# Planning a fifth slot early, casting the first slot's weights later, and reading the last routing first

## The chip, the cores and the metric

One core of a Trainium2 chip runs the whole program in one launch. The time is device microseconds of one execution, and the median of several is given. The engines are TensorE (PE, its weight loads apart as PEld), VectorE (DVE), ScalarE (ACT), GpSimd (POOL) and SyncE (SP), whose queue issues nearly all loads.

## The reference

Three stages follow one another.

1. Linear attention with a forget gate: 4 x 8 heads, 768 steps, head size 48. `state = f * state + k v^T`, `y = q state`.
2. A dense feed-forward over the 3072 tokens of 384 numbers: `h = x @ w_in` (384 x 2048), `g = softplus(h)`, `x2 = g @ w_out` (2048 x 384).
3. A mixture of eight experts. `logits = x2 @ w_gate + bias[modality]`; the largest names one expert of each token. A token's result is `p * (relu(x2 @ w1[e]) @ w2[e])`, with w1[e] 384 x 1024, w2[e] 1024 x 384 and p its softmax weight.

Counted with the reference on its inputs, the tokens by expert are 17, 281, 476, 430, 193, 956, 154, 181 after the first 2688 and 20, 327, 542, 487, 219, 1097, 167, 213 after all 3072.

## The kernel before, in words

**Tiling.** The tokens run in eight groups of 384 (NG = 8). Attention and dense layer are interleaved: a dense step `s` is one of 16 slices of 128 hidden units of one group, so there are 128 steps, numbered 0 to 127; step 112 is the first of the last group. Where exactness counts, a matrix of 32-bit numbers is split into a rounded part and a remainder (h and l, hi and lo): ScalarE casts, VectorE subtracts, and TensorE makes three matmuls of what would be one.

**A dense step** (the last group, steps 112 to 127). `up` (L573) makes 9 matmuls into PSUM, 384 columns each. `softplus` follows: abs (ACT L578), exp (ACT L579), two operations on DVE (L584, L585), the logarithm (ACT L586), two more on DVE (L587, L588); then `act2`: hi (ACT L612) and lo (DVE L613). `down` (L653) adds 9 matmuls into three banks `x2ps`, for the step two before.

**Routing.** When a group's last `down` is done, `route1` (L671 to L679) reads each bank j of `x2ps`: the logits `lg` on DVE (L674) and the row itself, `rows`, on ACT for j = 0 and 2 (L679) and on DVE for j = 1 (L677). `route2` then finds the expert and the row number and scatters the rows on POOL into a buffer `xs` in HBM that has a region for each expert (L724).

**Slots.** Afterwards the rows are worked off in slots: up to 256 rows of one expert with its whole weights. One slot is 8 blocks of `m_up` (block f: 9 matmuls L1115 into one of four PSUM buffers, relu `hh` on ACT L1117, remainder `hl` on DVE L1118), two halves of `m_down` (24 matmuls each, L1138) into a bank of `x2ps`, and `m_out`, which scales the result (ACT L1147) and scatters it on POOL (L1148). `m_T` transposes a slot's rows on TensorE (L1097) and splits them (ACT L1099, DVE L1100).

**Two plans.** The first NPRE slots are planned in step 116 (`plan_first`) from the seven groups that are complete by then; only whole blocks of 256 rows are taken. The rest is planned in slot 2 (`plan_rest`), after the last group's rows and the pad rows (`pad_rows`, L1209, eight transfers on POOL): NA slots of 256 rows and NSTAT in all, beside one "pair" slot. A branch at the end runs if more slots than that are needed. The numbers reach the loads by register reads on SP: the expert of a slot (L994), its first row (L982), the pair's experts (L1026). The rows of slot s are loaded by L984 into one of three buffers.

**Weights of a slot.** Eight transfers of 384 KB on SP (`raw`, L1008), in turn a quarter of w1 and a quarter of w2, each followed by a cast (ACT L1009) and a subtraction (DVE L1010). The first slot has two `raw` buffers, the others six. The first slot's transfers and casts are named in steps 117 to 124, one in each step; those of a later slot while the slot before it runs, beside its blocks. The weights of two slots fit at a time.

**Order.** Instructions are named in program order, which is their priority. A planner simulates the engines with its own costs and fixes each engine's order: the first ready by priority goes next. `follow(a, b)` puts a behind b in that order, without a wait on the chip. `at(s, f)` names f's work in step s. Each engine then runs its list strictly in order. After the dense steps the blocks 0 to 2 of slot 0 are named among the last parts of the dense layer, as `TAIL = "uaduue"` says (u: a block of slot 0, a: `act2` of the last step, d and e: the last two `down`). The buffers `lg` and `rows` of the last routing come from a pool (`gq`) that opens when the pool of the dense layer (`gp`), which also holds slot 0's operands, is closed.

```
    m_slots(seq, {(0, 3): final, (1, 2): lambda: route2(NG - 1), (1, 4): ready, (2, 2): then, (6, 3): limits})
```

This says that the last `route1` (`final`) is named behind block 3 of slot 0, and `plan_rest` (`then`) behind block 2 of slot 2.

Of the kernel before, what the change touches and what calls it, by code (L numbers as in the profile page):

```python
# [7 lines left out]
F32 = mybir.dt.float32  # L8
# [3 lines left out]
AF = mybir.ActivationFunctionType  # L12
ALU = mybir.AluOpType
# [5 lines left out]
NT, DM, DFF = 3072, 384, 2048  # L19
E, FE = 8, 1024  # L20
TG = 384
NG = NT // TG
# [2 lines left out]
NB = 16  # L25
SLOT = 256
CAP = NT + SLOT
NPRE = 4
NA = 8
NREST = 17  # L30
NSTAT = 10
HALF = 64
PAIRAT = 12
LEAN = 16
# [1 line left out]
PRE = 4  # L36
# [3 lines left out]
TAIL = "uaduue"  # L40
WPOS = 1
PADROW = E * CAP
PAIR0, PAIR1 = NF, NF * (NG - 1)
RW = 388
BIG = 65536.0
WS = 256.0
# [5 lines left out]
def moe_chain(ctx, tc, qT, kT, fT, vp, w_in, w_out, mod, w_gate, mbias, w1, w2, out):  # L52
    nc = tc.nc
# [23 lines left out]
    x2ps = [ps_x.tile([128, 512], F32, name=f"x2ps{j}") for j in range(3)]  # L77


    def follow(ins, other):  # L80

        tc.add_manual_dep(ins.ins, other.name,
                          mybir.DependencyInfo(mybir.DependencyClass.NoSync, mybir.DependencyReason.DATA),
                          reason="first steps first")
# [4 lines left out]
    marks = {}  # L89
# [315 lines left out]
    biasT = cp.tile([128, 24, 8], F32, name="biasT")  # L405
# [170 lines left out]
    def softplus(g, h, e, w, lean=False):  # L576

        ins = nc.scalar.activation(e, h, AF.Abs).ins  # L578
        nc.scalar.activation(e, e, AF.Exp, scale=-1.0)  # L579
        if lean:  # L580
            nc.scalar.activation(w, e, AF.Copy, bias=1.0)
            nc.vector.scalar_tensor_tensor(w, w, 1.0, e, op0=ALU.subtract, op1=ALU.subtract)
        else:
            nc.vector.tensor_scalar(w, e, 1.0, -1.0, op0=ALU.add, op1=ALU.add)  # L584
            nc.vector.tensor_tensor(w, w, e, op=ALU.subtract)  # L585
        nc.scalar.activation(e, e, AF.Ln, bias=1.0)  # L586
        nc.vector.scalar_tensor_tensor(e, h, 0.0, e, op0=ALU.max, op1=ALU.add)  # L587
        nc.vector.tensor_tensor(g, e, w, op=ALU.subtract)  # L588
        return ins
# [77 lines left out]
    def sm(nm, shape, dt=F32):  # L667
        return gp.tile(shape, dt, tag=nm, name=nm)

    def route1(G, j):  # L670
        if j == 0:  # L671
            rt[G] = {"lg": sm("lg", [128, 3, 8]), "rows": gp.tile([128, 3, RW], F32, tag="rows", name="rows", bufs=1)}
        lg, rows = rt[G]["lg"], rt[G]["rows"]
        nc.vector.scalar_tensor_tensor(lg[:, j, :], x2ps[j][:, DM:DM + 8], 1.0 / WS, biasT[:, 3 * G + j, :],  # L674
                                       op0=ALU.mult, op1=ALU.add)
        if j == 1:
            nc.vector.tensor_scalar(rows[:, j, 0:DM], x2ps[j][:, 0:DM], 1.0 / WS, None, op0=ALU.mult)  # L677
        else:
            nc.scalar.activation(rows[:, j, 0:DM], x2ps[j][:, 0:DM], AF.Copy, scale=1.0 / WS)  # L679

    def route2(G):
        d = rt[G]
# [52 lines left out]

    used = cp.tile([NREST, 8], F32, name="used")

    def pick(nm, num, w, offs):


        end, beg, oh, tmp, off = (cp.tile([NREST, w], F32, name=f"{x}{nm}") for x in ("end", "beg", "soh", "stmp", "off"))
        sel, row = (cp.tile([NREST, 1], F32, name=f"{x}{nm}") for x in ("sel", "row"))
        woff, roff = (cp.tile([NREST, 1], I32, name=f"{x}{nm}") for x in ("woff", "roff"))
        nc.vector.tensor_tensor_scan(end, num, zer[:, 0:w], 0.0, op0=ALU.add, op1=ALU.add)
# [10 lines left out]
        nc.vector.tensor_reduce(row, tmp, axis=AX.X, op=ALU.add)  # L755
        nc.vector.tensor_scalar(roff, row, float(PADROW), None, op0=ALU.add)
        return woff, roff, beg, end

    def counts(sh, add):
        p = ps_r.tile([128, 512], F32, tag="r", name="r")  # L760
        nc.tensor.matmul(p[:, 0:8], onesb, runb, start=True, stop=True)
        cf, ci = cp.tile([NREST, 8], F32, name=f"cf{sh}"), cp.tile([NREST, 8], I32, name=f"ci{sh}")
        nc.vector.tensor_copy(cf, p[0:NREST, 0:8])
        nc.vector.tensor_scalar(ci, cf, float(add), None, op0=ALU.add)
# [9 lines left out]
    def plan_first():  # L774
# [4 lines left out]
        woff, roff, beg, _ = pick("0", num, 8, rows0[:, 0:8])  # L779
        taken(used, beg, num, NPRE)  # L780
        return woff, roff
# [10 lines left out]
    def halves(num, offs):  # L792
# [15 lines left out]
        nc.vector.tensor_copy(pw, ph[:, :, 0])  # L808
        nc.vector.tensor_scalar(pr, ph[:, :, 1], float(PADROW), None, op0=ALU.add)
        return pw, pr  # L810

    def plan_rest():
# [12 lines left out]
        nc.vector.tensor_tensor(beg, end, num, op=ALU.subtract)  # L825
        taken(n16[:, 0:8], beg, num, NA)
        nc.vector.tensor_tensor(num, used, n16[:, 0:8], op=ALU.add)
# [11 lines left out]
    def limits():  # L839
# [4 lines left out]
        nc.vector.tensor_copy(nsl[:, 0:1], end)  # L844
        nc.vector.tensor_scalar(far, end, float(-NSTAT), 0.0, op0=ALU.add, op1=ALU.max)
        nc.vector.tensor_reduce(flm, fl, axis=AX.X, op=ALU.max)
# [34 lines left out]
    def at(s, f):  # L881
        extra.setdefault(s, []).append(f)
# [32 lines left out]
    for u in range(4, 33):  # L915
        G, j = divmod(u, 4)
        t = 3 * u - 10 if u < 8 else 4 * u - 19
# [74 lines left out]
    def m_weights(s, woff, i, whole):  # L992

        wo = nc.sync.value_load(woff[i:i + 1, 0:1], min_val=0, max_val=E - 1)  # L994
        pl = m1p[s % 2]
        names = ("w1h", "w1l", "w2h", "w2l")
        w1h, w1l, w2h, w2l = wts[s] = [pl.tile([128, 3 * FE], F32R, tag=n, name=n) for n in names]
        ops = []
        for n in range(4):
            for src, hi, lo in ((w1, w1h, w1l), (w2, w2h, w2l)):  # L1000
                def op(n=n, src=src, hi=hi, lo=lo):
                    c = slice(768 * n, 768 * n + 768)
                    rows = src[bass.ds(wo, 1), :, c].rearrange("o p f -> p (o f)")
                    if whole and src is w1:
                        nc.sync.dma_start(hi[:, c].bitcast(F32), rows)
                        return
                    t = rawp.tile([128, 768], F32, tag="raw", name="raw")
                    nc.sync.dma_start(t, rows)  # L1008
                    nc.scalar.copy(hi[:, c], t)  # L1009
                    nc.vector.tensor_tensor(lo[:, c], t, hi[:, c].bitcast(F32), op=ALU.subtract)  # L1010
                ops.append(op)
        return ops

# [88 lines left out]
    def m_up(s, f):  # L1102
        d = sl[s]
        t = d["t"]
        w1h, w1l = (t.rearrange("p (k f) -> p k f", k=3) for t in wts[s][0:2])
        if f == 0:
            d["hh"] = mp.tile([128, NF2, SLOT], F32R, tag="hh", name="hh")
            d["hl"] = mp.tile([128, NF2, SLOT], F32R, tag="hl", name="hl")
        if d["n"] == 2:
            hp = ps_h.tile([128, TG], F32, tag="h", name="h")  # L1110
            fs = slice(128 * f, 128 * f + 128)
            n = 0
            for kd in range(3):
                for w, x in ((w1h, 0), (w1h, 1), (w1l, 0)):
                    nc.tensor.matmul(hp[:, 0:SLOT], w[:, kd, fs], t[x][:, kd, :], start=(n == 0), stop=(n == 8))  # L1115
                    n += 1
            nc.scalar.activation(d["hh"][:, f, :], hp[:, 0:SLOT], AF.Relu)  # L1117
            nc.vector.scalar_tensor_tensor(d["hl"][:, f, :], hp[:, 0:SLOT], 0.0, d["hh"][:, f, :].bitcast(F32),  # L1118
                                           op0=ALU.max, op1=ALU.subtract)
        elif f % 2 == 0:  # L1120
            w1f = wts[s][0].bitcast(F32).rearrange("p (k f) -> p k f", k=3)
            hp = ps_h.tile([128, 2, 128], F32, tag="h", name="h")
            for i in range(2):
                fs = slice(128 * (f + i), 128 * (f + i) + 128)
                for kd in range(3):
                    nc.tensor.matmul(hp[:, i, :], w1f[:, kd, fs], t[:, kd, :], start=(kd == 0), stop=(kd == 2))
            hh, hl = d["hh"][:, f:f + 2, 0:128], d["hl"][:, f:f + 2, 0:128]
            nc.scalar.activation(hh, hp, AF.Relu)
            nc.vector.scalar_tensor_tensor(hl, hp, 0.0, hh.bitcast(F32), op0=ALU.max, op1=ALU.subtract)
# [25 lines left out]

    seq = [("first", i, 2) for i in range(NPRE)] + [("rest", i, 2 if i < NA else 1) for i in range(NSTAT)]
    seq.insert(PAIRAT, ("pair", 0, 1))
    more = [("rest", i, 1) for i in range(NSTAT, NREST)]
    plans = {}
# [46 lines left out]
    def pad_rows(e):  # L1206
# [5 lines left out]
            tc.declare_no_dep(ins, other, reason="rows of different experts")  # L1212
        pads.append(ins)

    def pre():
        plans["first"] = plan_first()
        for i in range(NPRE - 1):
            m_load(i, "first", i, 2)
        for n, op in enumerate(m_fetch(0, seq[0])):
            at(16 * (NG - 1) + PRE + 1 + n, op)  # L1220

    ffn(0, 16 * (NG - 1) + 3)
    for p in (ap1, ap2, ps_r, ps_h):
# [166 lines left out]
    with tc.If(rare > 0):  # L1390
        nv = nc.values_load(nsl[0:1, 0:1], min_val=0, max_val=NREST)
        with tc.If(nv > NSTAT):
            more = [(len(seq) + x, it) for x, it in enumerate(more)]
# [53 lines left out]
```

## Time and profile before

| | us |
|---|---|
| median of 3 runs (lowest, highest) | 816.93 (815.72, 817.48) |
| the profiled execution | 814.61 |
| its span | 812.9 |
| PE busy | 786.5 (97%) |
| PE weight loads busy | 730.8 (90%) |
| DVE busy | 633.5 (78%) |
| ACT busy | 530.4 (65%) |
| POOL busy | 64.9 (8%) |

The granted clock of TensorE is at its full level (2.4 GHz) in all slices of the page. Times in the views are microseconds from the span's start. The last group's dense steps lie at about 500 to 566 us, slot 0 runs until about 581 us, and each later slot of 256 rows takes some 17.6 us. A matmul's end is modelled, and the next one starts before it; idle time of an engine that isn't the bound costs nothing.

### The profile page before, as it was taken

What the parts mean: (1) busy time and instruction counts of PE and PEld (TensorE: products, weight loads), DVE (VectorE), ACT (ScalarE), POOL (GpSimd) and SP (SyncE); (2) the same over time, 40 slices, a digit from 0 to 9 for tenths busy, and PEclk for the clock granted to TensorE, in tenths of its full rate; (3) what the DMA queues carried; (4) which work ended last, traced back from release to release, by engine and by line L of the source; (5) the groups of instructions that cost most, each with busy time, mean ns of one, the idle gap of its engine ahead of it and who ended that gap; (6) DMA issues with size and microseconds to landing.
All of it is one profiled execution on the core that took longest, in us unless ns stands there. A gap on an engine that the chain in (4) does not pass through costs nothing.

```text
span 812.9 us, 16010 instructions
## 1 busy us (share of the span) xinstructions
PE 786.5 (97%) x5878; PEld 730.8 (90%) x5878; DVE 633.5 (78%) x1265; ACT 530.4 (65%) x1057; POOL 64.9 (8%) x86
## 2 busy tenths in 40 slices
PE   4899999999999999999999999999999999999997
PEld 4656568999999999999999999989999999999987
DVE  6899999998888888888888866888886766666131
ACT  5787797767766676777676665566775656655242
POOL 2000000200010010010010010100042111000010
PEclk9999999999999999999999999999999999999999
DMA  8794221321132132122221010055598976673980
GB/s 292 255 328 140 59 67 44 91 73 54 45 95 58 45 98 58 51 85 61 62 75 38 23 38 8 30 161 171 200 352 298 309 226 216 213 225 119 366 311 16
DMA packets 53976, 110.84 MB, mean 136 GB/s; under 512 B 7655, under 2 KB 27930, under 8 KB 53888
## 3 DMA queue, kind: packets, MB, share of 16 engines
q1 hardware_dynamic: 48768, 96.61, 37.2%
q0 software_dynamic: 4160, 12.67, 4.2%
q8 instruction: 48, 0.79, 0.4%
q10 hardware_dynamic: 960, 0.44, 0.2%
q14 instruction: 40, 0.33, 0.1%
HBM read 91.92 MB, written 13.65 MB: 130 GB/s over the span
## 4 chain that ended last, share of the span: by engine, by line
PE 49%; DVE 23%; ACT 10%; issue 10%; DMA 7%; SPq 1%; POOL 1%; POOLq 0%; DVEq 0%; ACTq 0%
PE x2ps L653 11%; PE h L573 11%; PE x2ps L1138 10%; PE h L1115 10%; DVE l L637 3%; DVE w L636 2%; DMA raw<-in_w_dram 2%; ACT e L633 1%; DVE f L110 1%; PE r L206 1%; ACT e L622 1%; DVE lo L640 1%; DVE am L214 1%; DVE l L639 1%; ACT r L623 1%
## 5 line engine op out<-in xcount | busy, mean ns | idle before, releaser
L573 PE MATMUL h<-xh,wih 128*128 128x384 f32 x336 | 118.4, 352 | 1.2 <-DVE e L587 1.2
L653 PE MATMUL x2ps<-woh,hi 128*128 128x392 f32 x336 | 115.3, 343 | 1.8 <-ACT hi L612 1.5
L653 PE MATMUL x2ps<-wol,hi 128*128 128x392 f32 x336 | 114.5, 341 | 0.0
L573 PE MATMUL h<-xh,wil 128*128 128x384 f32 x336 | 113.5, 338 | 0.0
L653 PE MATMUL x2ps<-woh,lo 128*128 128x392 f32 x336 | 113.4, 341 | 0.0
L573 PE MATMUL h<-xl,wih 128*128 128x384 f32 x336 | 113.3, 337 | 0.0
L1115 PE MATMUL h<-thl,w1h 128*128 128x256 f32 x528 | 96.5, 284 | 0.0
L1010 DVE TENSOR_TENSOR w2l<-raw,w2h 128x768 fp32r<-128x768 f32 x56 | 53.2, 951 | 38.8 <-ACT w2h L1009 18.0
L1115 PEld LDWEIGHTS h<-thl,w1h 128*128 128x128 f32 x528 | 82.0, 190 | 0.0
L638 ACT CAST hi<-l 128x768 fp32r<-128x768 f32 x48 | 40.0, 834 | 54.1 <-DVE l L637 42.5
L1115 PE MATMUL h<-thl,w1l 128*128 128x256 f32 x264 | 74.3, 282 | 0.0
L1138 PE MATMUL x2ps<-w2h,hh 128*128 128x384 f32 x208 | 71.0, 341 | 0.2 <-ACT rows L679 0.2
L1138 PE MATMUL x2ps<-w2h,hl 128*128 128x384 f32 x208 | 70.1, 337 | 0.8 <-DVE hl L1118 0.8
L1138 PE MATMUL x2ps<-w2l,hh 128*128 128x384 f32 x208 | 69.9, 336 | 0.0
L573 PEld LDWEIGHTS h<-xh,wih 128*128 128x128 f32 x336 | 63.0, 188 | 4.9 <-DVE e L587 2.0
L724 POOL DMA_INDIRECT xs<-rows,pos x24 | 27.1, 1129 | 504.4 <-DVE w L635 166.3
L653 PEld LDWEIGHTS x2ps<-woh,hi 128*128 128x128 f32 x336 | 63.0, 188 | 3.2 <-ACT hi L612 2.6
L653 PEld LDWEIGHTS x2ps<-woh,lo 128*128 128x128 f32 x336 | 63.0, 188 | 0.5
L573 PEld LDWEIGHTS h<-xl,wih 128*128 128x128 f32 x336 | 63.3, 188 | 0.0
L653 PEld LDWEIGHTS x2ps<-wol,hi 128*128 128x128 f32 x336 | 63.1, 188 | 0.0
L573 PEld LDWEIGHTS h<-xh,wil 128*128 128x128 f32 x336 | 63.0, 188 | 0.0
L1010 DVE TENSOR_TENSOR w1l<-raw,w1h 128x768 fp32r<-128x768 f32 x48 | 45.8, 954 | 21.9 <-ACT w1h L1009 21.3
(275 smaller groups left out, 1826.7 us busy)
## 6 DMA issues: line engine op xcount, KB each, us to landing
raw<-in_w_dram SPq DMA_DIRECT2D x104, 384.0 KB
f<-in_f_dram SPq DMA_DIRECT2D x28, 192.0 KB
k<-in_k_dram SPq DMA_DIRECT2D x28, 192.0 KB
q<-in_q_dram SPq DMA_DIRECT2D x28, 192.0 KB
xr<-xs SPq DMA_DIRECT2D x12, 388.0 KB
v<-in_v_dram SPq DMA_DIRECT2D x32, 144.0 KB
w1h<-in_w_dram SPq DMA_DIRECT2D x12, 384.0 KB
xf<-y SPq DMA_DIRECT2D x48, 72.0 KB
```

The source lines that it names most:

```text
L110: nc.vector.tensor_tensor_scan(d["f"], d["f"], clampt.to_broadcast([128, TG]), 1.0 if first else fl[:, n:n + 1], op0=ALU.mult, op1=ALU.min)
L206: nc.tensor.matmul(pa[h][:, cs], d["k"][64 * h:64 * h + 64, cs], d["q"][64 * h:64 * h + 64, cs], start=(c == 0), stop=True, skip_group_che ...
L214: marks["mask"] = nc.vector.tensor_tensor(am, pa[h][:, 0:TG].rearrange("p (c t) -> p c t", c=3), mask.unsqueeze(1).to_broadcast([128, 3, 1 ...
L573: nc.tensor.matmul(hp, w, x, start=(n == 0), stop=(n == len(terms) - 1))
L636: nc.vector.tensor_tensor(w, w, e, op=ALU.subtract)
L637: nc.vector.tensor_tensor(g, r, g, op=ALU.add)
L638: nc.scalar.copy(hi, g)
L653: nc.tensor.matmul(x2ps[j][:, 0:DM + 8], g[:, ts], w, start=(i == 0 and n == 0), stop=(i == NF - 1 and n == len(terms) - 1))
L724: ins = nc.gpsimd.indirect_dma_start(out=xs, out_offset=bass.IndirectOffsetOnAxis(ap=pos[:, j:j + 1], axis=0), in_=rows[:, j, :], in_offse ...
L1010: nc.vector.tensor_tensor(lo[:, c], t, hi[:, c].bitcast(F32), op=ALU.subtract)
L1115: nc.tensor.matmul(hp[:, 0:SLOT], w[:, kd, fs], t[x][:, kd, :], start=(n == 0), stop=(n == 8))
L1138: nc.tensor.matmul(acc[:, 0:DM], g[:, f, ts], w[:, f, :], start=(f == 0 and n == 0), stop=(f == NF2 - 1 and n == 2))
```

## The change

The first plan covers five slots instead of four, the second nine instead of ten (seven of them of 256 rows); the small tables grow from 17 to 18 rows. In the first slot the transfers stay in their steps 117 to 124, while cast and subtraction are named in steps 121, 121, 122, 123, 124, 124, 125 and 126, and each cast is put behind the logarithm of the step in which it is named. In blocks 4, 5 and 6 of slot 0 (LATE = 4), relu and remainder are put behind the reads that the last `route1` makes on the same engine of bank 0, 1 and 2.

```diff
-NPRE = 4
-NA = 8
-NREST = 17
-NSTAT = 10
+NPRE = 5
+NA = 7
+NREST = 18
+NSTAT = 9
+LATE = 4
@@ softplus
-        nc.scalar.activation(e, e, AF.Ln, bias=1.0)
+        marks["log"] = nc.scalar.activation(e, e, AF.Ln, bias=1.0).ins
@@ route1
-        nc.vector.scalar_tensor_tensor(lg[:, j, :], x2ps[j][:, DM:DM + 8], 1.0 / WS, biasT[:, 3 * G + j, :],
-                                       op0=ALU.mult, op1=ALU.add)
+        ins = [nc.vector.scalar_tensor_tensor(lg[:, j, :], x2ps[j][:, DM:DM + 8], 1.0 / WS, biasT[:, 3 * G + j, :],
+                                              op0=ALU.mult, op1=ALU.add)]
         if j == 1:
-            nc.vector.tensor_scalar(rows[:, j, 0:DM], x2ps[j][:, 0:DM], 1.0 / WS, None, op0=ALU.mult)
+            ins.append(nc.vector.tensor_scalar(rows[:, j, 0:DM], x2ps[j][:, 0:DM], 1.0 / WS, None, op0=ALU.mult))
+            eng = (0, 0)
         else:
-            nc.scalar.activation(rows[:, j, 0:DM], x2ps[j][:, 0:DM], AF.Copy, scale=1.0 / WS)
+            ins.append(nc.scalar.activation(rows[:, j, 0:DM], x2ps[j][:, 0:DM], AF.Copy, scale=1.0 / WS))
+            eng = (0, 1)
+        marks["route"] = [(j, e, x) for e, x in zip(eng, ins)] + [y for y in marks["route"] if y[0] != j]
@@ m_weights, op
                     nc.sync.dma_start(t, rows)
-                    nc.scalar.copy(hi[:, c], t)
-                    nc.vector.tensor_tensor(lo[:, c], t, hi[:, c].bitcast(F32), op=ALU.subtract)
+                    def parts():
+                        ins = nc.scalar.copy(hi[:, c], t)
+                        if not s:
+                            follow(ins, marks["log"])
+                        nc.vector.tensor_tensor(lo[:, c], t, hi[:, c].bitcast(F32), op=ALU.subtract)
+                    if s:
+                        parts()
+                    else:
+                        return parts
@@ m_up
-            nc.scalar.activation(d["hh"][:, f, :], hp[:, 0:SLOT], AF.Relu)
-            nc.vector.scalar_tensor_tensor(d["hl"][:, f, :], hp[:, 0:SLOT], 0.0, d["hh"][:, f, :].bitcast(F32),
-                                           op0=ALU.max, op1=ALU.subtract)
+            two = [None, nc.scalar.activation(d["hh"][:, f, :], hp[:, 0:SLOT], AF.Relu)]
+            two[0] = nc.vector.scalar_tensor_tensor(d["hl"][:, f, :], hp[:, 0:SLOT], 0.0, d["hh"][:, f, :].bitcast(F32),
+                                                    op0=ALU.max, op1=ALU.subtract)
+            if s == 0 and f >= LATE and f < LATE + 3:
+                for j, e, x in marks["route"]:
+                    if j == f - LATE:
+                        follow(two[e], x.ins)
@@ pre
-        for i in range(NPRE - 1):
+        for i in range(3):
             m_load(i, "first", i, 2)
         for n, op in enumerate(m_fetch(0, seq[0])):
-            at(16 * (NG - 1) + PRE + 1 + n, op)
+            at(16 * (NG - 1) + PRE + 1 + n, lambda op=op: turn.append(op()))
+            at(16 * (NG - 1) + PRE + 5 + 3 * n // 4, lambda: turn.pop(0)())
```

## Rows read from the trace of the kernel before

**Rows 1.** Stretches: us, busy PE PEld DVE ACT POOL, clock, DMA share, GB/s.
```profile
530.00:566.00 36.00, 34.40 (x202) 32.88 (x202) 30.68 (x58) 23.92 (x47) 0.00 (x0) 1.00 0.60 187
539.00:558.00 19.00, 17.63 (x103) 16.55 (x102) 18.23 (x32) 14.90 (x28) 0.00 (x0) 1.00 0.48 129
566.00:580.00 14.00, 13.28 (x90) 12.84 (x89) 9.18 (x31) 8.34 (x17) 0.98 (x1) 1.00 0.22 70
580.00:632.00 52.00, 51.21 (x377) 50.64 (x376) 41.43 (x114) 34.12 (x64) 14.52 (x17) 1.00 0.92 326
632.00:800.00 168.00, 167.92 (x1348) 163.88 (x1347) 90.83 (x150) 90.66 (x172) 19.82 (x20) 1.00 0.71 236
```

**Rows 2.** TensorE's timeline, dense steps: start, us, line, op, [idle before <-releaser].
```profile
540.61 0.34 PE L573 MATMUL h<-xl,wih 128*128 128x384 f32 x1
540.78 0.34 PE L573 MATMUL h<-xh,wil 128*128 128x384 f32 x1
542.35 0.45 PE L653 MATMUL x2ps<-woh,hi 128*128 128x392 f32 x1 [1.22 <-ACT hi L612]
```

**Rows 3.** TensorE's timeline, first slot's blocks and start of its down part.
```profile
560.96 0.36 PE L1115 MATMUL h<-th,w1h 128*128 128x256 f32 x1
...
566.04 0.34 PE L653 MATMUL x2ps<-woh,lo 128*128 128x392 f32 x1
...
570.81 0.28 PE L1115 MATMUL h<-tl,w1h 128*128 128x256 f32 x1
570.93 0.28 PE L1115 MATMUL h<-th,w1l 128*128 128x256 f32 x1
571.71 0.44 PE L1097 MATMUL r<-ident,xr 128*128 128x128 f32 x2 [0.50 <-DVE thl L1100]
572.36 0.44 PE L1138 MATMUL x2ps<-w2h,hh 128*128 128x384 f32 x1 [0.22 <-ACT rows L679]
```

**Rows 4.** TensorE's timeline, end of slot 3.
```profile
630.57 0.44 PE L1138 MATMUL x2ps<-w2h,hl 128*128 128x384 f32 x1 [0.79 <-DVE hl L1118]
```

**Rows 5.** Chain of waits, 525 to 545 us: start, us, what.
```profile
532.69 5.41 DMA raw<-in_w_dram
```

**Rows 6.** ScalarE's timeline, dense steps: weight casts (L1009), a logarithm (L586).
```profile
538.12 0.83 ACT L1009 CAST w1h<-raw 128x768 fp32r<-128x768 f32 x1 [1.88 <-DMA raw<-in_w_dram]
538.86 0.52 ACT L586 ACTIVATE e<-e 128x384 f32<-128x384 f32 x1
...
543.22 0.83 ACT L1009 CAST w1h<-raw 128x768 fp32r<-128x768 f32 x1
...
554.04 0.84 ACT L1009 CAST w1h<-raw 128x768 fp32r<-128x768 f32 x1
```

**Rows 7.** VectorE's timeline, the same place.
```profile
536.74 0.55 DVE L613 TENSOR_TENSOR lo<-e,hi 128x384 fp32r<-128x384 f32 x1
538.99 0.96 DVE L1010 TENSOR_TENSOR w1l<-raw,w1h 128x768 fp32r<-128x768 f32 x1 [1.70 <-ACT w1h L1009]
539.86 0.55 DVE L587 SCALAR_TENSOR_TENSOR e<-h,e 128x384 f32<-128x384 f32 x1
```

**Rows 8.** ScalarE's timeline, blocks of the first slot and the last routing reads.
```profile
567.95 0.39 ACT L1117 ACTIVATE hh<-h 128x256 fp32r<-128x256 f32 x1 [0.67 <-PE h L1115]
...
570.35 0.58 ACT L1099 CAST thl<-r 128x512 fp32r<-128x512 f32 x1
...
571.82 0.49 ACT L679 ACTIVATE rows<-x2ps 128x384 f32<-128x384 f32 x1 [0.20 <-DVE lg L674]
```

**Rows 9.** ScalarE's timeline, slot 3: a cast of slot 4's weights.
```profile
625.69 0.84 ACT L1009 CAST w1h<-raw 128x768 fp32r<-128x768 f32 x1 [1.16 <-DMA raw<-in_w_dram]
```

**Rows 10.** Waits of SP's queue, 590 to 640 us: total, times, longest.
```profile
SPq L1026 <- DVE sel L749: 13.8, 1, 13.8
```

**Rows 11.** POOL's timeline, slot 2.
```profile
611.49 1.02 POOL L1148 DMA_INDIRECT out_dram<-o,xr  x1 [0.30 <-issue]
```

**Rows 12.** SP's timeline: the load of slot 4's rows.
```profile
616.73 0.33 SPq L984 DMA_DIRECT2D xr<-xs  x1
```

More of the change, by code (lines that the diff above doesn't have):

```diff
@@ L668, in sm @@
         return gp.tile(shape, dt, tag=nm, name=nm)
+    marks["route"] = []
     def route1(G, j):
@@ L1213, in pad_rows @@
         pads.append(ins)
+    turn = []
     def pre():
         plans["first"] = plan_first()
-        for i in range(NPRE - 1):
+        for i in range(3):
             m_load(i, "first", i, 2)
         for n, op in enumerate(m_fetch(0, seq[0])):
-            at(16 * (NG - 1) + PRE + 1 + n, op)
+            at(16 * (NG - 1) + PRE + 1 + n, lambda op=op: turn.append(op()))
+            at(16 * (NG - 1) + PRE + 5 + 3 * n // 4, lambda: turn.pop(0)())
     ffn(0, 16 * (NG - 1) + 3)
```

## The prediction

> **What bounds the kernel now.** I read the table of stretches first, because the change touches four places and each has its own limit. TensorE is the bound of the slots: from 632 to 800 us it is idle for 0.08 us in all [rows 1]. So the change can only give back TensorE's gaps in the stretches that it touches. These are 36.00 - 34.40 = 1.60 us between 530 and 566 us (the last dense steps, where the first slot's weights are cast), 0.72 us between 566 and 580 us (end of the first slot's blocks, last routing reads), and 0.79 us between 580 and 632 us, all of it at one place, the end of slot 3 [rows 1].
>
> Next I went into the timeline of TensorE. A matmul is drawn 0.34 us long but the next one starts 0.17 us later [rows 2], so a gap that is drawn costs about 0.16 us more than it shows. The largest one: 540.78 to 542.35 us is 1.57 us from start to start, less 0.17, which is 1.40 us lost for 1.22 us drawn. The first stretch holds three such gaps (1.22 us is the first, the other two make up the remaining 0.38), so it loses 1.60 + 3 x 0.16 = 2.08 us. In the second stretch 570.93 to 571.71 us loses 0.78 - 0.12 = 0.66 us, and the two transposes from 571.71 to 572.36 us take 0.65 us where about 0.27 is their own: 0.38 us [rows 3]. At 630.57 us 0.79 + 0.16 = 0.95 us is lost [rows 4]. All that the change can aim at is 2.08 + 1.04 + 0.95 = 4.07 us, 0.5% of the time.
>
> Then I asked what each gap waits for. The first: the transfer of the first weight chunk takes 5.41 us [rows 5], ScalarE stands 1.88 us in front of its cast at 538.12 us, and the logarithm of a dense step (538.86 us) waits behind it [rows 6]; VectorE has nothing to do meanwhile and stands 1.70 us [rows 7]. The second: VectorE's part of slot 1's operand and the copy of the routing rows at 571.82 us [rows 3, 8]. The third: casts of slot 4 that wait for transfers (1.16 us at 625.69 us), which began late because the queue on SP stood 13.8 us in front of a number of the second plan [rows 9, 10].
>
> **The change part by part.** The profiled execution took 814.61 us, 2.32 us less than the median of 816.93 (span 812.9 and 1.7 around it). I work out differences there and put them on the median.
>
> *Amount of work.* Five and nine slots instead of four and ten: the same twelve slots of 256 rows, two of 128 and the pair, so nothing is added on TensorE. That holds only if seven groups fill five whole blocks of 256 rows. Counting experts with the reference on its inputs gives 281, 476, 430 and 956 tokens for four experts after 2688 tokens and under 256 for the others: 1 + 1 + 1 + 3 = 6 blocks. For all 3072 tokens the rest is 7 whole blocks and 2 singles, which are exactly the nine planned. One row more in small tables costs nothing.
>
> *Casts four dense steps later.* The eight transfers keep their steps; the casts move behind the logarithm of the step four later, two or three steps later for the last ones. There are still two raw buffers, so only two transfers can run ahead; the third waits for the first subtraction, as now. The pace stays: first cast 538.12, third 543.22, seventh 554.04 us [rows 6], 5.1 to 5.4 us for each pair. What changes is what stands behind a waiting cast. The step whose logarithm stood at 538.86 us has its inputs ready when VectorE ends at 537.3 us at the latest, so it runs 1.5 us or more earlier, ahead of the first cast, and its two VectorE operations of 0.55 us [rows 7] fall into the 1.70 us in which VectorE stood. The matmul at 542.35 us is then free in time. What is late next is VectorE itself: from 539 to 558 us it is busy 18.23 of 19 us [rows 1], and the subtractions (8 x 0.96 us) stay. So only idle time that VectorE can fill comes back: 2 x 0.55 = 1.1 us, little more. I take 1.2 us gained. Ends: all 2.08 us gained; or 1.4 us lost, if one more cast stands in front of its transfer as the first does now.
>
> The Trainium skill (Perfetto Trace Analysis, Identifying the Most-Contended Engine) says to judge VectorE by its busy share, and TensorE by that of its weight loads and not of its matmuls. From 539 to 558 us these are 96% against 16.55 of 19 us, 87%. By this rule VectorE limits that stretch and a change that takes no work off it gains what it fills of its idle time, 1.1 us; by TensorE's gaps alone it would be 2.08 us, and the whole sum 0.9 us larger.
>
> Cover of the later casts: blocks from the third one on need the last chunk of w1, whose subtraction ends at 554.04 + 0.84 + 0.96 = 555.8 us; the third block runs at 560.96 us [rows 3]. This leaves 5.1 us, about 3 when TensorE arrives 2 us sooner, so a shift of one dense step (18 matmuls of 0.17 us, 3.1 us) costs nothing. The last chunk of w2 is needed only in the down part, after 572 us.
>
> *Routing reads ahead of blocks 4 to 6.* Their inputs are complete soon after the matmul at 566.04 us, but the copy runs at 571.82 us [rows 3, 8]: the planner opens the buffers of the reads only after those of the first slot's operands close, that is behind the last block. Naming them first changes the order on ScalarE and VectorE: relu (0.39 us [rows 8]) and subtraction of blocks 4, 5 and 6 stand behind the reads. The four PSUM buffers hold blocks 4 to 7 meanwhile, so TensorE goes on. But the operand cast at 570.35 us needs transposes that run between blocks 6 and 7, and if the planner keeps it ahead of the copies, they come at 571.5 instead of 571.82 us. I take 0.3 us gained. Ends: 1.04 us gained, if the copies run near 567 us in the gap that ScalarE has there; 0.5 us lost, if down waits for relus that now come after the copies.
>
> *The fifth planned slot.* Slot 4 takes its expert and rows from the first plan, so SP doesn't stand 13.8 us before its transfers. Its first two can go as soon as slot 3's last subtractions free the ring, while SP now still stands. Then comes its row load, which needs the row buffer of slot 1. That slot's second output is issued on POOL only at 611.49 us and takes 1.02 us there [rows 11]; with some 4 to 5 us to land (an estimate from the 5.41 us of [rows 5]) the row load and the six transfers behind it start near 617 us, no earlier than the row load does now (616.73 us) [rows 12]. Still, two of eight transfers are then done before it, in a stretch whose DMA engines are nearly full (0.92 of the time from 580 to 632 us [rows 1]), and that is worth more than the 1.16 us that is missing. The wait for the second plan moves to slot 5, whose transfers follow slot 4's anyhow, when the plan is long there. I take 0.9 us gained; ends 0.95 gained and 0.95 lost (the same gap one slot later besides).
>
> Sum: 1.2 + 0.3 + 0.9 = 2.4 us: 812.2 us in a profiled execution, **814.5 us** on the median. All lower ends give 816.93 - 4.07 = 812.9 us, all upper ends 816.93 + 2.85 = 819.8 us.
>
> **The rivals.** *A, forecast:* 814.5 us, chance 0.46.
>
> *B, only the plan's wait goes:* VectorE's full queue turns the cast gaps into as many small ones, and the copies stay behind the operand cast. For it: 18.23 of 19 us busy, and nothing taken off. Against it: the 1.70 us of idle time at 538 us is plainly caused by the order. 816.93 - 0.9 = 816.0 us, chance 0.28.
>
> *C, all gaps go:* 812.9 us, chance 0.12. For it: the four gaps have causes that the change names one by one. Against it: the full VectorE, the row load of slot 4.
>
> *D, slower: a cast waits in front of every pair.* With two raw buffers a transfer starts only after the subtraction two before. If dense steps run ahead of the transfers, ScalarE stands before the first cast of each of four pairs as it now stands once, and every time TensorE loses 1.40 us: 4 x 1.40 = 5.6 in place of 2.08 us, with the 0.9 us of slot 4 gained, +2.6 us, 819.5 us. It decides from the third such wait: two cost 2.8 against 2.08 + 0.9 us gained. For it: the pace of 5.1 to 5.4 us per pair is longer than a dense step. Against it: the casts are named one to two steps apart, which is about that pace. Chance 0.11.
>
> *E, it doesn't do what it says* (fifth slot empty, ten slots left, the extra branch runs): at least one slot more, 8 blocks of 9 matmuls of 0.12 us and 48 of 0.17 us [rows 2, 3], about 17 us, near 834 us. The count of six blocks excludes it but for an error of mine: 0.03.
>
> **How the numbers follow.** About 0.2% (1.6 us) is what a measurement of this kernel can tell from no change. Faster (under 815.3 us): C, and A but for its edge, with some of B: 0.58. Same: B mostly and A's edge: 0.28. Slower: D, E and a little of B's far side: 0.14. The range of 8 in 10 runs from C's 812.9, less 0.2 us, to 817.7 us, between B and D; A's own range is 813.3 to 815.6 us.
>
> **What would show it.** Right: no idle time of ScalarE over 1 us before a cast near 538 us, VectorE's 1.70 us gap shorter by 1.1 us or more, TensorE idle under 0.9 us in the last dense steps; the row copies before the relus of blocks 4 to 6; no wait of 13.8 us ahead of slot 4's transfers, and no gap in slot 3's down part. Wrong: gaps of TensorE that wait for the subtraction's VectorE queue or for hi in steps behind the first pair (B, D), a gap before the third block of the first slot, or the down part of slot 0 waiting for relus of blocks 4 to 6.

## The result: slower, 825.34 us against 816.97

The changed kernel takes 825.34 us (median of 6, 822.58 to 829.88) against 816.97 us for the kernel before, run beside it: ratio 1.0105, 95% interval 1.0076 to 1.0134. I had forecast 814.5 us, and the time is outside my range. The profiled execution took 823.88 us (span 822.2).

The same stretches as in [rows 1], of the kernel after (us, busy PE PEld DVE ACT POOL, clock, DMA share, GB/s):

```profile
530.00:566.00 36.00, 34.05 (x198) 31.96 (x197) 29.49 (x55) 23.52 (x46) 0.00 (x0) 1.00 0.58 187
539.00:558.00 19.00, 18.01 (x101) 16.41 (x100) 15.86 (x30) 14.17 (x26) 0.00 (x0) 1.00 0.42 115
566.00:580.00 14.00, 13.44 (x91) 12.82 (x90) 8.58 (x32) 7.76 (x19) 0.63 (x1) 1.00 0.10 26
580.00:632.00 52.00, 46.37 (x330) 45.58 (x330) 39.84 (x109) 32.59 (x59) 14.40 (x17) 0.94 0.93 317
632.00:800.00 168.00, 167.91 (x1342) 163.88 (x1341) 91.88 (x152) 91.26 (x173) 19.00 (x19) 1.00 0.75 243
```

The loss is in one row: from 580 to 632 us TensorE stands 5.63 us instead of 0.79, and this row alone has a granted clock under 1.00. It is one stop, in slot 3's up part (TensorE's timeline; start, us, line, [idle before <-releaser]):

```profile
622.55 0.28 PE L1130 MATMUL h<-thl,w1l 128*128 128x256 f32 x1
628.46 0.79 PE L1130 MATMUL h<-thl,w1h 128*128 128x256 f32 x2 [5.63 <-DVE hl L1133]
```

VectorE's subtraction waits for the relu on ScalarE. ScalarE's timeline shows why the relu is late; it answers to [rows 9]:

```profile
614.70 0.36 ACT L1114 CAST thl<-r 128x256 fp32r<-128x256 f32 x1
622.36 0.83 ACT L1017 CAST w1h<-raw 128x768 fp32r<-128x768 f32 x1 [7.30 <-DMA raw<-in_w_dram]
625.05 0.83 ACT L1017 CAST w1h<-raw 128x768 fp32r<-128x768 f32 x1 [1.86 <-DMA raw<-in_w_dram]
625.79 0.57 ACT L1166 ACTIVATE o<-x2ps,xr 128x384 f32<-128x384 f32 x1
626.26 0.82 ACT L1017 CAST w2h<-raw 128x768 fp32r<-128x768 f32 x1
626.99 0.39 ACT L1132 ACTIVATE hh<-h 128x256 fp32r<-128x256 f32 x1
```

ScalarE stands 7.30 and 1.86 us in front of casts of slot 4 whose transfers have not landed, and slot 3's first relu (626.99 us) is queued behind them. TensorE fills the four PSUM buffers and stops. The kernel before took slot 4's casts no sooner (the fifth at 625.69 us, after a wait of 1.16 us [rows 9]) and lost 0.95 us [rows 4]: there most relus stood ahead of the casts or between them, the last one ahead of the last two casts. Two more rows of its ScalarE timeline, the third cast and the last relu:

```profile
622.40 0.84 ACT L1009 CAST w1h<-raw 128x768 fp32r<-128x768 f32 x1 [0.89 <-DMA raw<-in_w_dram]
...
627.91 0.40 ACT L1117 ACTIVATE hh<-h 128x256 fp32r<-128x256 f32 x1
```

So the third transfer is there at about 622.4 us in both kernels; what differs is what stands behind its cast. The Trainium skill (PSUM — Partial Sum Buffer, Engine vs sequencer instructions) says that ScalarE's queue is strictly first in, first out; the trace agrees: the first relu's input was ready at about 619.6 us, when the ninth matmul of its block had ended, and it ran only behind the cast that stood 7.30 us and the ones after it.

Why the transfers are late is in the chain of waits (start, us, what):

```profile
594.70 6.87 DMA xs<-rows,pos
...
611.74 0.06 POOL xs L1228
...
613.03 1.16 issue
614.19 3.18 DMA out_dram<-o,xr
617.50 0.33 SPq L990
...
619.25 5.78 DMA raw<-in_w_dram
...
626.36 0.73 ACT w2h L1017
...
628.46 3.57 PE h L1130 x15
```

Read it upwards from the stop. Slot 4's transfer starts behind the row load (L990), which needs slot 1's row buffer. That is free when slot 1's second output has left, and this output is issued on POOL behind eight pad writes:

```profile
602.28 2.90 POOL L1228 DMA_DIRECT2D xs<-padt  x4 [6.60 <-DMA xs<-rows,pos]
...
611.73 0.68 POOL L1228 DMA_DIRECT2D xs<-padt  x1 [1.13 <-issue]
612.71 1.17 POOL L1167 DMA_INDIRECT out_dram<-o,xr  x1 [0.30 <-issue]
614.19 1.02 POOL L1167 DMA_INDIRECT out_dram<-o,xr  x1 [0.30 <-issue]
```

The wait of 13.8 us on the plan [rows 10] is gone, and another stands in its place (waits of SP's queue, 600 to 640 us: total, times, longest):

```profile
SPq L990 <- DMA out_dram<-o,xr: 14.9, 2, 12.6
```

Slot 3 lasts 25.20 us (618.41 to 643.61) instead of 18.56 (616.67 to 635.23), 6.64 more. The stop is 628.46 - 622.55 - 0.12 = 5.79 us, 4.84 over the old 0.95; the rest of the 6.64, 1.8 us, I put down to the clock (3.9 us at half of it are worth 1.95). It fell during the stop and stayed at 0.50 (1.2 GHz) for some 3.9 us after TensorE had started again (same columns as above):

```profile
624.00:626.00 2.00, 0.00 (x0) 0.00 (x0) 0.90 (x8) 0.95 (x2) 0.00 (x0) 0.88 1.02 369
626.00:628.00 2.00, 0.00 (x0) 0.00 (x0) 1.76 (x3) 2.00 (x5) 1.09 (x1) 0.50 0.65 220
...
631.00:632.00 1.00, 1.00 (x6) 1.00 (x6) 1.00 (x3) 0.41 (x2) 0.00 (x0) 0.50 0.24 95
632.00:633.00 1.00, 1.00 (x9) 1.00 (x8) 1.00 (x3) 0.38 (x1) 0.00 (x0) 0.82 0.55 89
633.00:634.00 1.00, 1.00 (x11) 1.00 (x10) 0.54 (x2) 0.32 (x2) 0.00 (x0) 1.00 0.94 363
```

At 0.50 there are 6 or 7 matmuls in a microsecond, at 1.00 there are 11.

Of the 9.27 us between the two profiled executions 6.64 are slot 3's. TensorE's idle time changes by +0.35 us in the dense steps and by -0.16 at the first slot's end; 0.75 us are there at 530 us, before the first changed instruction. 0.9 us lie behind the last matmul (from its start to the span's end 6.66 us instead of 5.75). The rest, 0.8 us, I cannot place: the kernel before alone varied from 813.29 to 820.14 us in one series of runs.

### The profile page after: what moved, and what is told of

It is laid out like the page before. It is cut to its first block, busy times and chain, and to the rows that moved or that the text cites. A ratio compares the mean times of both kernels' runs of the same rounds, so it can differ in the third digit from the quotient of the medians.

```text
span 822.2 us, 16010 instructions
## 1 busy us (share of the span) xinstructions
PE 789.2 (96%) x5878; PEld 732.4 (89%) x5878; DVE 633.4 (77%) x1265; ACT 530.4 (65%) x1057; POOL 64.1 (8%) x86
## 4 chain that ended last, share of the span: by engine, by line
PE 52%; DVE 18%; issue 16%; ACT 6%; DMA 6%; POOL 1%; POOLq 1%; SPq 1%; DVEq 0%; ACTq 0%
PE h L574 14%; PE x2ps L654 14%; PE h L1130 8%; PE x2ps L1157 8%; PE r L207 2%; PE r L195 1%; PE r L183 1%; DVE l L638 1%; DVE f L111 1%; DVE w L637 1%; DMA f<-in_f_dram 1%; DVE am L215 1%; POOL out_dram L1167 1%; DVE e L588 1%; DMA woh_raw<-in_w_in_dram 1%
## 5 line engine op out<-in xcount | busy, mean ns | idle before, releaser
L1130 PE MATMUL h<-thl,w1h 128*128 128x256 f32 x528 | 98.3, 287 | 5.6 <-DVE hl L1133 5.6
```

## The experiments

Every time is set beside that of the kernel before on the same chip (its medians lay between 815.75 and 817.00 us). "Stop" is idle time of TensorE as the timeline draws it.

**The three parts one by one.** The fifth slot alone is four constants and `range(3)`; the other two are the rest of the diff, each by itself.

> The kernel before with the fifth planned slot alone. Theory 1 (slot 4's row load stands on SP in front of its weight transfers until slot 1's output has left, and ScalarE stands in front of slot 4's casts with slot 3's relus behind them): the whole loss is here, TensorE stops 5 to 6 us at about 621 us, slot 3 takes about 25 us instead of 18.6, the time is 7 us above before (822.5 to 825). Rival 2 (the stop needs the shifts that the other two parts bring, the slot alone is harmless): within 1.5 us of before. Rival 3 (my prediction's term): 0.9 us faster.

823.33 us, ratio 1.0095 (1.0080 to 1.0109), 7.2 us slower. The stop and its cause are there without the other parts:

```profile
619.21 0.84 ACT L1009 CAST w1h<-raw 128x768 fp32r<-128x768 f32 x1 [6.29 <-DMA raw<-in_w_dram]
...
625.32 0.80 PE L1115 MATMUL h<-thl,w1h 128*128 128x256 f32 x2 [4.61 <-DVE hl L1118]
```

Theory 1 stands as to the place; rivals 2 and 3 fall.

> The kernel before with the first slot's casts four dense steps later, four planned slots. Theory 1, which puts the loss into the fifth slot: the trace after has 2.76 us of stops of TensorE between 530 and 566 us against 2.08 before, so 0 to 1 us slower, no stop over 1.5 us. Rival 2 (this part carries a good share of the 8.4 us): 2 us slower or more. My prediction's term: 1.2 us faster.

816.88 us, ratio 1.0006 (0.9994 to 1.0018): no difference. The 1.22 us gap of [rows 2] is gone, as I had predicted, and the subtractions that moved back now stand ahead of an operand that a later block of the first slot needs:

```profile
547.78 0.45 PE L653 MATMUL x2ps<-woh,hi 128*128 128x392 f32 x1 [0.28 <-ACT hi L612]
...
564.04 0.38 PE L1124 MATMUL h<-tl,w1h 128*128 128x256 f32 x1 [0.77 <-DVE tl L1109]
```

TensorE idles 1.26 us between 530 and 566 us where it idled 1.60: the part gains 0.3 us there, not 1.2. Between 539 and 558 us TensorE's idle time falls from 1.37 to 0.38 us and VectorE is busy 16.83 us instead of 18.23 [rows 1]; the work and most of the idle time come back behind 558 us.

> The kernel before with the routing reads ahead of blocks 4 to 6 of the first slot, nothing else. Theory 1: the stops at the first slot's end go from 1.04 to about 0.9 us, no difference that can be measured (within 0.5 us of before). Rival 2: the reads push blocks 4 to 6 back and the down part waits, 0.5 us slower or more. Rival 3 (the drift of 0.75 us that the changed kernel has before its first changed step comes with this order): 0.7 us slower with the stops unchanged.

815.92 us, ratio 0.9998 (0.9987 to 1.0009): no difference, and the stops at the first slot's end add up to 0.88 us instead of 1.04.

**Which cause makes the stop.** First the row load, moved on SP behind six transfers.

```
-            op = ops[2]
-            ops[2] = lambda: (m_load(s, where, i, n), op())
+            x = 6 if s == 4 else 2
+            op = ops[x]
+            ops[x] = lambda: (m_load(s, where, i, n), op())
```

> The changed kernel with slot 4's row load moved on SP behind six of its eight weight transfers. Theory 1: the transfers go out as the ring of raw buffers frees, from about 601 us on, ScalarE doesn't stand before slot 4's casts, the stop of 5.8 us goes: 6 to 7 us faster than the changed kernel, 816.5 to 819 us. Rival 2 (the transfers themselves are late because the DMA engines are full, the row load only happens to stand there): a stop of 3 us or more stays at the same place, 821 us or more. Rival 3 (the order of the casts ahead of the relus alone makes the stop): it stays too, whatever the transfers do.

825.55 us, ratio 1.0114 (1.0099 to 1.0128): nothing gained. The edit was too short: the last w1 chunk is the seventh transfer, it is still behind the row load, and ScalarE stands before its cast, 7.46 us at 626.78 us. But the casts ahead of it show something new: they stand 3.08 and 3.06 us although no row load holds their transfers. So I took the row load's wait away, and separately the order.

```
+        xr = gp.tile([128, 2, RW], F32, tag="x4", name="x4") if s == 4 else xrp.tile(...)
-NOUT = 15
+NOUT = 13
```

> The changed kernel with a row buffer of its own for slot 4 (two output buffers fewer), so that its row load needn't wait for slot 1's output. Theory 1 (row load ahead of the transfers): no wait of over 10 us at that load on SP, all transfers of slot 4 asked for before 613 us, the stop of 5.8 us falls below 1.5 us, 818 to 820 us. Rival 2 (full DMA engines: in the run with the row load moved the casts before it still stood 3.1 us each in front of their transfers): casts still stand 3 us each, the stop stays at 3 us or more, 821 us or more.

821.16 us, ratio 1.0070 (1.0051 to 1.0089). The row load goes at 602.49 us, and still ScalarE waits:

```profile
615.25 0.83 ACT L1017 CAST w1h<-raw 128x768 fp32r<-128x768 f32 x1 [5.46 <-DMA raw<-in_w_dram]
619.17 0.83 ACT L1017 CAST w1h<-raw 128x768 fp32r<-128x768 f32 x1 [3.09 <-DMA raw<-in_w_dram]
...
620.80 1.23 PE L1130 MATMUL h<-thl,w1h 128*128 128x256 f32 x2 [3.96 <-ACT thl L1114]
```

Its DMA view (600 to 612 us; KB each, median us from issue to landing) tells why: transfers that are asked for early run beside the pads.

```profile
xs<-padt POOLq DMA_DIRECT2D x8, 388.0 KB, 8.3
raw<-in_w_dram SPq DMA_DIRECT2D x7, 384.0 KB, 11.3
```

By the marks set beforehand this is rival 2: casts stand 3 us and more, and the stop is 3.96 us. Taking the row load's wait away gives back a part at most: the ratio goes from 1.0105 to 1.0070, and the two intervals overlap.

The order alone, `follow(ins, marks["relu"])` behind each cast of slot 4, where `marks["relu"]` is slot 3's relu of the same step:

> The changed kernel with each cast of slot 4 named behind one relu of slot 3, so that ScalarE takes relu, cast, relu, cast, as the kernel before nearly does; row load and transfers as in the changed kernel. Theory 3 (late transfers cost only by the relus that stand behind a waiting cast): the transfers land as late as in the changed kernel, the stop falls below 1.5 us, 818 to 820 us. Theory 1 alone (whoever stands first, the transfers come too late for slot 4): the stop moves to slot 3's down part or slot 4's first blocks and stays over 3 us, 821 us or more.

822.63 us, ratio 1.0082 (1.0061 to 1.0104). The stop moves to slot 3's down part: now the last relu stands behind late casts (at 630.36 and 634.53 us, after waits of 2.15 and 2.85).

```profile
635.70 0.69 PE L1161 MATMUL x2ps<-w2h,hh 128*128 128x384 f32 x1 [4.60 <-ACT hh L1134]
```

The place is that of theory 1, but its cause is not the row load alone. The casts of the first six transfers stand 1.41 us at most; the seventh transfer goes only at 627.03 us, though a buffer was free at about 621.7. From 620.15 us on SP reads numbers of the second plan into registers, eleven in a row ahead of it (one line of the code on SP: count, ns min/median/max, first to last start):

```profile
L1000 SPq TENSOR_LOAD <-woff x6: 267/270/272, 620.1 to 626.2; - x6
L988 SPq TENSOR_LOAD <-roff x6: 264/268/277, 620.8 to 627.4; - x6
```

So this run does not test the order by itself, and in the kernel before the last relu stood ahead of the last two casts; that order was not run with five planned slots.

The same two cures without the other parts of the change:

> The kernel before with the fifth planned slot and slot 4's own row buffer, without the late casts and the early routing reads. Theory 1: no stop over 1.5 us in slot 3, 815.5 to 817 us (0.9 us gained at the end of slot 3, nothing given up in the dense steps). Rival 2 (full DMA engines): a stop of 3 us or more, 819 us or more.

820.95 us, ratio 1.0062 (1.0039 to 1.0086), with a stop of 3.29 us.

> The kernel before with the fifth planned slot and each cast of slot 4 behind one relu of slot 3. Theory 3 (the order on ScalarE): no stop over 1.5 us in slot 3, 815.5 to 817.5 us, no more than 0.5 us from the run with its own row buffer. Theory 1 alone: a stop of 3 us or more, 819 us or more.

823.89 us, ratio 1.0101 (1.0075 to 1.0127), with a stop of 5.38 us in slot 3's down part; here too the seventh transfer (630.42 us) stands behind a row of register reads, twelve from 622.5 to 630.1 us. Neither cure is enough as it was built.

**Both cures, or the pads elsewhere.** Own row buffer and order together; then, instead of them, `(1, 4): ready` becomes `(2, 4): ready`, which names the pads one slot later.

> The changed kernel with both edits at once: slot 4's own row buffer, and each of its casts behind one relu of slot 3. Theory 4 (two causes in a row: slot 4's transfers, asked for early, run beside the pad writes on full DMA engines and take 10 to 14 us; and their casts stand ahead of slot 3's relus. With the row buffer alone 4.1 us were still lost, with the order alone 4.8 us): the transfers land between 615 and 624 us and are taken as they come, no stop over 1 us in slot 3, 816.5 to 818.5 us. Rival (either cause alone is enough to cost 4 us): a stop of 3 us or more, 820 us or more.

819.83 us, ratio 1.0047 (1.0028 to 1.0067). Six of slot 4's casts run without a wait, the seventh stands 4.20 us at 629.01 us, the next w1 cast 0.92 us at 631.24 us, and TensorE 2.82 us behind them. The seventh transfer was issued at 625.45 us though its buffer was free at about 620. What stood in SP's queue is no wait: it is the same reads, for all later slots in a row:

```profile
629.01 0.83 ACT L1017 CAST w1h<-raw 128x768 fp32r<-128x768 f32 x1 [4.20 <-DMA raw<-in_w_dram]
```

```profile
L1000 SPq TENSOR_LOAD <-woff x7: 267/270/1333, 615.2 to 624.7; - x7
```

With their partners (L988) and one for the pair slot (L1043) they fill SP from 613.3 to 625.2 us. I take it that the planner puts them there because it sees SP idle while a transfer waits for its buffer; no run shows this.

> The changed kernel with the eight pad writes named one slot later (from slot 2's fifth block on instead of slot 1's), all else as it is, the casts of slot 4 ahead of slot 3's relus too. Theory 4: slot 1's output leaves at about 602 us instead of 614, the row load goes at about 606 instead of 617.5, slot 4's transfers run without the pads beside them (5 to 6 us each instead of 10 to 14) and land before 616 us; no stop in slot 3; 816.5 to 818.5 us. Rival (the order on ScalarE is wrong by itself): a stop of 3 us or more stays in slot 3. Rival (the pads only move the crush): the stop comes one slot later, at slot 5's weights, 3 us or more.

819.24 us, ratio 1.0038 (1.0021 to 1.0055). The row load goes at 605.33 us as expected, but the pads, now issued from 605.98 to 618 us, still lie beside slot 4's transfers; casts stand 2.4 to 4.0 us, the stop is 1.99 us.

> The kernel before with the fifth planned slot and the pad writes one slot later, without the late casts and the early routing reads. Theory 4: no stop over 1 us after 580 us, 815 to 816.5 us, so 0 to 0.9 us faster than before. Rival (the crush moves to slot 5): 819 us or more.

819.51 us, ratio 1.0039 (1.0020 to 1.0058): same as the run before, so the other two parts neither cause nor cure it.

> The same with the early routing reads added. Theory 4: 0.1 to 0.4 us below the run without them, which is not to be told from it; 815 to 816.5 us. Rival: as there.

819.31 us, ratio 1.0032 (1.0013 to 1.0050).

**The pads behind slot 4's transfers**, `(3, 0): ready`.

> The changed kernel with the pad writes named at slot 3's first block, so that they leave after slot 4's transfers; the order of casts and relus in slot 3 is that of the changed kernel. Theory 4: slot 4's transfers take 5 to 6 us and land before 614 us, ScalarE stands under 1 us in front of each cast, no stop over 1 us in slot 3; pads run from about 618 to 636 us and hold slot 5's row load, whose casts the planner then names among slot 4's relus, so the stop there stays under 1 us: 815.5 to 817 us. Rival (casts ahead of relus cost by themselves): 2 us or more stop in slot 3, 818.5 us or more. Rival (the crush moves on with the pads): a stop of 2 us or more in slot 4, 818.5 us or more.

819.13 us, ratio 1.0028 (1.0009 to 1.0047). Slot 3 has no stop left, though five of slot 4's casts still stand ahead of slot 3's first relu (four in the changed kernel). So casts ahead of relus cost nothing there when their transfers have landed:

```profile
600.00:620.00 20.00, 20.00 (x149) 19.88 (x148) 18.43 (x71) 14.39 (x27) 3.01 (x3) 1.00 0.78 268
620.00:640.00 20.00, 20.00 (x149) 19.96 (x148) 8.50 (x16) 7.56 (x17) 7.56 (x10) 1.00 0.77 269
640.00:660.00 20.00, 17.78 (x126) 17.30 (x125) 15.02 (x24) 14.76 (x28) 1.95 (x2) 1.00 0.94 325
```

and its transfers land quickly (DMA view, 600 to 613 us):

```profile
raw<-in_w_dram SPq DMA_DIRECT2D x9, 384.0 KB, 4.4
```

4.4 us against 11.3, for seven transfers beside the eight pads, is the price of the pads, and that part of theory 4 is shown. The price goes by how much is asked for at once: in the run with the order alone three transfers between 600 and 612 us, beside the same pads, took 5.6 us in the median. But the last rival is right too: slot 4 now has two stops.

```profile
641.93 0.50 PE L1130 MATMUL h<-thl,w1h 128*128 128x256 f32 x2 [1.02 <-DVE hl L1133]
...
644.90 0.50 PE L1130 MATMUL h<-thl,w1h 128*128 128x256 f32 x2 [1.20 <-DVE hl L1133]
```

Two of slot 5's transfers go at 618.56 and 619.49 us, the other six only from 635.57 us on, behind the row load at 634.97. The row load stood behind register reads, which fill SP from 619.9 to 634.3 us.

> The kernel before with the fifth planned slot and the pad writes at slot 3's first block, without late casts and early routing reads. Theory 4: 815 to 816.5 us, so between no change and the 0.9 us that I had forecast. Rivals as in the run before: 818.5 us or more, with the stop in slot 3 or in slot 4.

820.45 us, ratio 1.0042 (1.0021 to 1.0062).

> The same with the early routing reads. Theory 4: within 0.4 us of the run without them, 814.7 to 816.5 us. Rivals: 818.5 us or more.

819.54 us, ratio 1.0036 (1.0017 to 1.0055). Neither comes near what theory 4 expected; stops in slot 4 again (1.01 and 0.94 us, then 2.94), and in the second run 0.89 us in slot 3.

**Slot 5's row load later too** (`x = 5 if s == 5 else 2`, as in the first edit above):

> The kernel before with the fifth planned slot, the routing reads early, the pads at slot 3's first block and slot 5's row load behind five of that slot's weight transfers. Theory 4 (a row load that waits for other writes stands on SP in front of transfers that wait for nothing): no stop over 1 us after 580 us, 815 to 816.5 us. Rival (the DMA engines are overfull wherever the pads stand): 1.5 us or more of stops in slots 3 to 5, 818 us or more.

824.43 us, ratio 1.0091 (1.0069 to 1.0114), far from what was expected, with 5.89 us of stop in slot 4. SP's hold here is no wait; it reads, two numbers for each of nine slots, the first at 621.3 us and the others from 625.7 to 642 us, and slot 5's last three transfers stand behind the reads:

```profile
L1000 SPq TENSOR_LOAD <-woff x9: 266/517/909, 621.3 to 640.8; - x9
...
L988 SPq TENSOR_LOAD <-roff x9: 268/627/1071, 625.7 to 641.4; - x9
```

```profile
647.26 0.83 ACT L1015 CAST w2h<-raw 128x768 fp32r<-128x768 f32 x1 [7.53 <-DMA raw<-in_w_dram]
...
649.47 0.80 PE L1121 MATMUL h<-thl,w1h 128*128 128x256 f32 x2 [5.89 <-DVE hl L1124]
```

So the theory that the row load's wait for the pads was the whole rest falls; the reads are enough to hold these transfers.

> The same without the early routing reads: within 0.4 us of it. Rival as there.

822.62 us, ratio 1.0068 (1.0047 to 1.0089), with a stop of 5.87 us in slot 4.

> As the first, with the pads one block earlier, at slot 2's last block. Theory 4: the last pads land some 2 us earlier and leave slot 5 more room, while slot 4's last transfers have two or three pads beside them: 815 to 817 us, stops under 1 us each. Rival: 818 us or more, with stops of 1 us and more in both slots 3 and 4.

821.65 us, ratio 1.0075 (1.0050 to 1.0101), with a stop of 3.58 us in slot 4.

No version with five planned slots comes back to the kernel before; the nearest is the one with the pads behind slot 4's transfers, 0.28% above. Left open: a version that names each slot's reads just ahead of its own transfers was not run, so whether five slots could then give the 0.9 us is not known.

## Why the prediction was wrong, step by step

*The fifth planned slot: -0.9 us forecast, +7.2 us measured by itself.* This is the step that failed. Its facts were right: two transfers go early (603.19 and 604.39 us), then the row load stands until near 617 us, behind slot 1's output on POOL, and the other six start at 618. The failure is the sentence after that, "two of eight transfers are then done before it ... and that is worth more than the 1.16 us that is missing", and the upper end of 0.95 us that I took from the kernel before. I compared when the transfers start, and did not ask what stands behind their casts on ScalarE. In the kernel before, slot 4's casts stood among slot 3's relus; in the changed kernel four of them stand ahead of the first relu, while on the chip the third transfer is as late as before (its cast at 622.36 us against 622.40). A late transfer now costs 5.79 us of stop where it cost 0.95. Why the planner moved the casts is not shown: my reading is that it had modelled the wait for the plan, which is gone, and does not model the wait behind the pads on POOL. Late transfers and this order together make the loss: the kernel before had the one without the other and lost 0.95 us, and with the pads behind slot 4's transfers the order stands, the transfers are in time, and slot 3 has no stop.

*The DMA engines.* I had the full stretch (0.92) as an argument for starting early. The runs show the opposite sign: seven transfers that start beside the pads take 11.3 us instead of 4.4. In the changed kernel only two start there, so its loss did not come from this; the run with slot 4's own row buffer ran into it.

*The clock* is a term that I did not have: about 1.8 us of the 6.64.

*The casts: -1.2 us forecast, no difference measured (-0.5 to +1.5 us).* The step that moved was right (the large gap goes), the size was not: 1.2 us was mis-sized and measured 0.3 us by the trace. VectorE's work is only moved, and 0.77 us come back before a later block of the first slot. No difference lies within the bounds that I gave (2.08 us gained to 1.4 lost), which are wide. In the changed kernel the cast still stands, 1.73 us at 539.92 us, but the logarithm is ahead of it; my mark "no idle time over 1 us before a cast" was the wrong thing to look for.

*The routing reads: -0.3 us forecast, -0.2 us measured (-1.1 to +0.7), -0.16 us by the stops.* The time cannot tell this from nothing; by the stops the direction is right and the size about half. It is right too that the operand cast stays ahead of the copies (571.96 and 573.44 us).

*The rivals.* D had the right kind of mechanism (casts that stand before their transfers) in the wrong slot. E did not happen. No case of mine had a price for slot 3 over 0.95 us, so the range could not hold the result.

## What to carry to other kernels

When a change lets work be ordered earlier, ask whether what it waits for is earlier on the chip too, and what will now stand behind it: on an engine that runs its list in order, the order sets what a late transfer costs (5.79 us here against 0.95). A bound for a moved transfer is not the old gap; it is the time until everything queued behind its first reader can run. Before transfers are started earlier, look at what else uses the DMA engines then, and at everything in the issuing queue, register reads among it.

## What I had not expected of the hardware

Reads of single numbers into SP's registers cost 0.26 to 0.27 us while the DMA engines are quiet (DMA share 0.04 from 621 to 623 us in the run with both cures), and 0.52 to 0.63 us in the median in the run whose reads lie beside pads and transfers (the longest in any of these runs, 1.60 us). With what follows each of them 19 in a row held the queue for 16 us (625.7 to 642.1 us), 0.86 us for each. The Trainium skill (DMA: Bandwidth & Descriptors, Latency and other measured facts) gives about 600 ns as the floor of such a load; here such a read takes 0.26 to 0.27 us when the DMA engines are quiet, so the measurement decides against it.

After a stop of 5.63 us the clock stays at its lower level for some 3.9 us of work, which adds about 1.8 us to the stop. After the stop of 2.82 us in the run with own row buffer and order together it was 0.50 from 632 to 634 us; after 1.99 us in the run with the pads one slot later, and in the run with two stops of 1.02 and 1.20 us, it stayed at 1.00.
